# Moving one bf16 permutation from VectorE to GpSimd, behind a gate, and two matmuls ahead of a stage

## The chip, the cores and the metric

One core of a Trainium2 chip. The metric is device time of one execution in microseconds (us). Engines: PE is TensorE (PEld its weight loads), DVE is VectorE, ACT is ScalarE, POOL is GpSimd, SP is SyncE, whose queue issues transposing DMAs and output stores.

## The reference

Two attention steps for 8 batches of 8 heads (sequence 576, head size 64, 32 packed queries), then a two-layer block with h*cos(h):

```python
p_packed = sm_attn(p, k, v)              # 32 packed queries per head
out = sm_attn(q, p_packed, p_packed)     # 576 queries per head
x = out.transpose(0, 2, 1, 3).reshape(B * S, H * D)
h = x @ w_in                             # 512 -> 2048
g = h * np.cos(h)
return g @ w_out                         # 2048 -> 512
```

## The kernel before

The kernel runs as a pipeline over batches. Batch s has a *stage* of 16 chunks: for each chunk, four hidden matmuls, a cosine on ScalarE and a product on VectorE. Output matmuls of batch s-1 are spread between the chunks as filler. Also in the stage, v of batch s+1 is permuted (`permute_v`) and multiplied with its attention weights (`pp`); `ppw` and `pw2` multiply that product with w_in. PSUM is the memory that matmuls write; a *bank* or *buffer* of it is free again when its content has been read. Ahead of each stage, ScalarE and VectorE normalise the probabilities (`a2n`) that the hidden matmuls read.

```python
A = ctx.enter_context(tc.tile_pool(name="psA", bufs=3, space=PSUM))   # ring of 3: chunks, pp, ppw
O = ctx.enter_context(tc.tile_pool(name="psO", bufs=2, space=PSUM))   # output banks
...
def permute_v(b, eng=G):
    vp[b] = vp_pool.tile([TP, C, H * D], BF16, name="vp", tag="vp")
    copy(eng, vp[b]..., bf["v", b]...)                # 96 x 3072, bf16
...
def normalise(b):
    ...                                                # ScalarE: exp(-ln(sum)) for y = 0, 1
    for y in range(2):
        V.scalar_tensor_tensor(out=a2n[b][:, y], in0=a2u[b][:, y], scalar=r1[b][:, y:y + 1],
                               in1=lns[b][:, y], op0=ALU.mult, op1=ALU.mult)
...
def h_mm(b, fc):                                       # one chunk
    ps = psa()
    for y in range(2):
        for e in range(2):
            nc.tensor.matmul(ps[:, e, 0:HS], PPW[b]..., a2n[b][:, y, ...], ...)
    ACT.activation(out=csv, in_=ps[:, :, 0:HS], func=AF.Sin, bias=PI_HALF)
    def rest():
        V.tensor_tensor(out=gT[b][:, fc, :]..., in0=ps[:, :, 0:HS], in1=csv, op=ALU.mult)
        ...
...
def slot(s, hooks, keep=0, heavy={}):                  # the stage
    left = filler[1] - keep
    out_eng[:] = (ACT,) if s > 1 else (V, ACT)
    for fc in range(NFC):
        h_mm(s, fc)()
        quota = ...                                    # share of `left` due after this chunk
        ...                                            # hooks of chunk fc run here, then fill(...)
...
ppw(2, 3, V)
normalise(2)
ACT.preload_act_table_set(SIN_SET)
fill(8)                                                # output matmuls
G.tensor_copy(out=gate, in_=xT["k", 4][0:1, 0, 0:1])   # holds the loads until k4 is transposed
for n, b in (("v", 4), ("q", 4), ("k", 5)):
    load(n, b)
fill(5)
slot(2, [(4, lambda: permute_v(3, V)), (7, lambda: pp(3, engs=(ACT, ACT))), (11, lambda: pw2(3))], 5, {11: 3})
```

The softmax here doesn't subtract the row's maximum and nothing guards it: scores larger than these inputs give would overflow.

## Time and profile before

250.03 us median of 6 runs (249.93 to 250.45). The first part of the profile's page gives busy time per engine and the share of the span:

```profile
PE 234.5 (94%) x2003; PEld 131.6 (53%) x2037; DVE 168.0 (68%) x254; ACT 166.9 (67%) x278; POOL 54.8 (22%) x68
```

PE bounds the kernel, so only time in which PE waits can be saved.

The timeline of batch 2's stage, before (columns: start in us, duration in us, engine, line, operation, output<-input and shapes, count; in brackets the engine's idle time and what ended it):

```profile
75.00 2.49 PEld L309 LDWEIGHTS <-gT 128*128 128x128 bf16 x13 [0.42 <-issue]
75.23 2.75 PE L309 MATMUL ot<-w_out_bf,gT 128*128 128x512 bf16 x12 [0.16 <-issue]
76.02 1.28 ACT L495 ACT_TABLE_LOAD   x1
77.20 1.54 DVE L243 SCALAR_TENSOR_TENSOR a2n<-a2u,r,lns 128x576 bf16<-128x576 bf16 x2
78.07 0.41 PE L256 MATMUL psA<-a2n,PPW 128*128 128x288 bf16 x2
78.80 0.41 PE L256 MATMUL psA<-a2n,PPW 128*128 128x288 bf16 x2 [0.32 <-DVE a2n L243]
...
83.92 0.95 DVE L77 COPY vp<-vbf 96x3072 bf16<-96x3072 bf16 x1
84.35 0.65 PE L256 MATMUL psA<-a2n,PPW 128*128 128x288 bf16 x4
84.78 2.08 DVE L263 TENSOR_TENSOR gT<-psA,cosT 128x576 bf16<-128x576 f32 x3
85.58 0.86 PE L183 MATMUL psA<-a1T,vp 96*128 96x64 bf16 x24 [0.58 <-DVE gT L263]
...
95.65 1.28 ACT L505 ACT_TABLE_LOAD   x1
```

At the head, the hidden matmuls need the two normalise instructions (L243, ending at 78.01 and 78.74): the first pair runs at 78.07, the second at 78.80. At `pp` (L183), the matmuls need a free buffer of the three-buffer PSUM ring. The one due is that of chunk 5, whose product was the first of the three at 84.78, ended at 85.53, and had the permutation in front of it in VectorE's queue.

To size a wait I take the distance between two matmul starts in the trace and subtract what the first costs when nothing waits (0.12 us for 288 columns, 0.213 for 512; uninterrupted neighbours in this trace start 0.122 and 0.216 us apart). That gives 0.73 us at the head (0.24 ahead of the first pair, 0.49 ahead of the second) and 0.74 us at pp. The two ScalarE table loads (76.02 and 95.65) bracket the stage: 19.63 us. I call this the *stage time*.

### The profile page before, as it was taken

What the parts mean: (1) busy time and instruction counts of PE and PEld (TensorE: products, weight loads), DVE (VectorE), ACT (ScalarE), POOL (GpSimd) and SP (SyncE); (2) the same over time, 40 slices, a digit from 0 to 9 for tenths busy, and PEclk for the clock granted to TensorE, in tenths of its full rate; (3) what the DMA queues carried; (4) which work ended last, traced back from release to release, by engine and by line L of the source; (5) the groups of instructions that cost most, each with busy time, mean ns of one, the idle gap of its engine ahead of it and who ended that gap; (6) DMA issues with size and microseconds to landing.
All of it is one profiled execution on the core that took longest, in us unless ns stands there. A gap on an engine that the chain in (4) does not pass through costs nothing.

```text
span 248.2 us, 5035 instructions
## 1 busy us (share of the span) xinstructions
PE 234.5 (94%) x2003; PEld 131.6 (53%) x2037; DVE 168.0 (68%) x254; ACT 166.9 (67%) x278; POOL 54.8 (22%) x68
## 2 busy tenths in 40 slices
PE   8878799999999899999999999999999999999993
PEld 3454374566544654475546554565456554665452
DVE  2549987789568967678857766678766774876110
ACT  2368799746566787888877777888787684873000
POOL 8333533240400044022313105030500000000000
PEclk9999999999999999999999999999999999999999
DMA  6999999999899999999989995989491113201133
GB/s 91 203 203 206 205 206 229 200 241 153 162 206 219 167 158 220 206 193 173 190 162 192 174 194 68 177 164 209 103 156 33 45 42 82 47 26 58 46 83 85
DMA packets 63175, 37.09 MB, mean 149 GB/s; under 512 B 35792, under 2 KB 58576, under 8 KB 63152
## 3 DMA queue, kind: packets, MB, share of 16 engines
q0 software_dynamic: 23152, 18.75, 49.5%
q1 hardware_dynamic: 39568, 17.83, 34.3%
q8 instruction: 16, 0.26, 0.4%
q10 hardware_dynamic: 432, 0.20, 0.4%
q14 instruction: 7, 0.06, 0.1%
HBM read 37.22 MB, written 9.44 MB: 188 GB/s over the span
## 4 chain that ended last, share of the span: by engine, by line
PE 75%; DMA 9%; DVE 7%; ACT 5%; issue 2%; SPq 0%; DVEq 0%; ACTq 0%
PE ot L309 42%; PE psA L256 19%; DMA qbf<-in_q_dram 7%; DVE gT L263 4%; PE psA L207 3%; PE ot L347 3%; PE psA L183 2%; ACT cosT L260 2%; DMA out_dram<-osb 2%; PE psA L129 2%; PE ot L295 1%; PE psA L233 1%; DVE PPW L77 1%; ACT ppT L75 1%; PE psA L104 1%
## 5 line engine op out<-in xcount | busy, mean ns | idle before, releaser
L309 PE MATMUL ot<-w_out_bf,gT 128*128 128x512 bf16 x482 | 127.4, 379 | 2.1 <-issue 1.3
L263 DVE TENSOR_TENSOR gT<-psA,cosT 128x576 bf16<-128x576 f32 x128 | 93.6, 755 | 26.5 <-ACT cosT L260 25.9
L260 ACT ACTIVATE cosT<-psA 128x576 bf16<-128x576 f32 x128 | 82.5, 652 | 28.0 <-PE psA L256 23.2
L256 PE MATMUL psA<-a2n,PPW 128*128 128x288 bf16 x512 | 83.8, 286 | 1.9 <-DVE PPW L77 0.4
L309 PEld LDWEIGHTS <-gT 128*128 128x128 bf16 x512 | 47.7, 98 | 43.2 <-issue 6.7
L256 PEld LDWEIGHTS <-PPW 128*128 128x128 bf16 x512 | 49.3, 98 | 35.2 <-issue 4.4
L77 DVE CAST PPW<-psA 128x1024 bf16<-128x1024 f32 (+1 forms) x23 | 26.9, 1176 | 11.6 <-PE psA L207 11.5
L267 POOL COPY joint<-gT 128x512 bf16<-128x512 bf16 x16 | 9.8, 614 | 88.5 <-DVE gT L263 88.5
L77 DVE COPY osb<-ot 128x512 f32<-128x512 f32 (+1 forms) x24 | 16.3, 679 | 17.5 <-PE ot L309 7.6
L75 ACT COPY osb<-ot 128x512 f32<-128x512 f32 (+1 forms) x13 | 7.3, 565 | 15.3 <-PE ot L309 10.6
L77 POOL COPY vp<-vbf 96x3072 bf16<-96x3072 bf16 x6 | 16.5, 2751 | 3.8 <-DMA vbf<-in_v_dram 3.8
L243 DVE SCALAR_TENSOR_TENSOR a2n<-a2u,r,lns 128x576 bf16<-128x576 bf16 x16 | 12.3, 814 | 7.3 <-ACT lns L241 7.3
L140 ACT ACTIVATE a<-psA 128x576 bf16<-128x576 f32 x16 | 10.3, 647 | 7.1 <-PE psA L129 7.1
L235 ACT ACTIVATE lns<-psA 128x576 f32<-128x576 f32 x16 | 10.2, 650 | 7.1 <-PE psA L233 6.5
L309 PE MATMUL ot<-w_out_bf,joint 128*128 128x512 bf16 x46 | 12.4, 379 | 0.1
L225 ACT ACTIVATE a2u<-psA,rs 128x576 bf16<-128x576 f32 x16 | 11.0, 737 | 1.4 <-PE psA L129 1.3
L75 ACT CAST ppT<-psA 64x128 bf16<-64x128 f32 x24 | 6.2, 260 | 7.2 <-DVE ppT L77 5.9
L207 PE MATMUL psA<-w_in_bf,ppT 64*32 64x512 bf16 x224 | 10.2, 381 | 0.0
L347 PE MATMUL ot<-wz 128*128 128x512 bf16 x23 | 8.7, 524 | 1.4 <-DVE wz L358 1.2
L241 ACT ACTIVATE lns<-lns 128x576 f32<-128x576 f32 x16 | 10.0, 676 | 0.0
L183 PEld LDWEIGHTS <-vp 96*128 96x128 bf16 x192 | 6.6, 98 | 2.2 <-issue 1.1
L77 DVE COPY kT<-psA 128x768 bf16<-128x768 bf16 x8 | 4.2, 552 | 5.2 <-PE psA L104 5.1
(72 smaller groups left out, 150.8 us busy)
## 6 DMA issues: line engine op xcount, KB each, us to landing
kbf<-in_k_dram POOLq DMA_DIRECT2D x8, 576.0 KB, 12.0
vbf<-in_v_dram POOLq DMA_DIRECT2D x8, 576.0 KB, 7.3
qbf<-in_q_dram POOLq DMA_DIRECT2D x8, 576.0 KB, 9.6
out_dram<-osb SPq DMA_DIRECT2D x24, 192.0 KB, 2.6
out_dram<-osb SPq DMA_DIRECT2D x22, 128.0 KB, 2.4
w_in_bf<-in_moe_w_in_dram POOLq DMA_DIRECT2D x4, 512.0 KB, 17.5
w_out_bf<-in_moe_w_out_dram POOLq DMA_DIRECT2D x4, 512.0 KB, 20.4
out_dram<-osb SPq DMA_DIRECT2D x26, 64.0 KB, 2.1
```

Source lines behind the costliest of these rows:

```text
L75: ACT.copy(out=out, in_=in_)
L77: eng.tensor_copy(out=out, in_=in_)
L140: ACT.activation(out=a1[b % 2][:, y, :, 0:TP].rearrange("p (e m) x -> p e m x", e=2), in_=ps[y][:, :, 0:HS].rearrange("p e (m x) -> p e m ...
L183: nc.tensor.matmul(ps[:, hp * 64:(hp + 1) * 64], vp[b][:, c, hp * 128:(hp + 1) * 128], a1T[b][0:TP, :, j, 32 * hp:32 * hp + 32], start=(j ...
L207: nc.tensor.matmul(ps[y][32 * x:32 * x + 32, :], ppT[b % 2][r, 2 * x + y, :], w_in_bf[r, x, n * 512:(n + 1) * 512], start=True, stop=True)
L225: ACT.activation(out=a2u[b][:, y].rearrange("p (e x) -> p e x", e=2), in_=ps[y][:, :, 0:HS], func=AF.Exp, scale=rs1[b][:, y:y + 1])
L243: V.scalar_tensor_tensor(out=a2n[b][:, y], in0=a2u[b][:, y], scalar=r1[b][:, y:y + 1], in1=lns[b][:, y], op0=ALU.mult, op1=ALU.mult)
L256: nc.tensor.matmul(ps[:, e, 0:HS], PPW[b][:, y, fc * 128:(fc + 1) * 128], a2n[b][:, y, e * HS:(e + 1) * HS], start=(y == 0), stop=(y == 1))
L260: ACT.activation(out=csv, in_=ps[:, :, 0:HS], func=AF.Sin, bias=PI_HALF)
L263: V.tensor_tensor(out=gT[b][:, fc, :].rearrange("p (e x) -> p e x", e=2), in0=ps[:, :, 0:HS], in1=csv, op=ALU.mult)
L309: nc.tensor.matmul(pss[c], w, w_out_bf[:, fc, :], start=(fc == 0), stop=(fc == NFC - 1))
L347: nc.tensor.matmul(wps, wz[:, 0:128], wz, start=True, stop=True)
```

## The change

GpSimd is otherwise idle here, so the permutation goes there. A one-element copy that reads the second normalised half holds GpSimd back until the normalise is over. Two output matmuls are taken from the stage and put ahead of it, so that 15 instead of 13 stand behind the normalise.

```diff
@@ -494,11 +494,13 @@
     normalise(2)
     ACT.preload_act_table_set(SIN_SET)
     fill(8)
+    G.tensor_copy(out=gate, in_=a2n[2][0:1, 1, 0:1])
+    permute_v(3)
     G.tensor_copy(out=gate, in_=xT["k", 4][0:1, 0, 0:1])
     for n, b in (("v", 4), ("q", 4), ("k", 5)):
         load(n, b)
-    fill(5)
-    slot(2, [(4, lambda: permute_v(3, V)), (7, lambda: pp(3, engs=(ACT, ACT))), (11, lambda: pw2(3))], 5, {11: 3})
+    fill(7)
+    slot(2, [(7, lambda: pp(3, engs=(ACT, ACT))), (11, lambda: pw2(3))], 5, {11: 3})
```

## The prediction

> **What bounds the kernel.** TensorE. The page's first part has PE busy 94% of a 248.2 us span, VectorE and ScalarE 67 to 68%; the chain that ended last is 75% PE; the clock is 1.00. In the timeline, matmuls follow each other almost without gaps (0.216 us per 128x512 output matmul, 0.122 us per 128x288 hidden matmul), so only a PE gap can be saved. Batch 2's stage (78 to 97 us) has two:
>
> 1. Head. The 13 output matmuls behind the normalise end at 78.04. The first two hidden matmuls (y=0) run at 78.07; the y=1 pair waits until 78.80 for the second normalise on VectorE, which ended at 78.74. Stall 0.49 us.
> 2. The pp matmuls of batch 3 could start at 84.84 and start at 85.58: 0.74 us. They need the PSUM buffer of hidden chunk 5, whose VectorE product ran at 84.78 to 85.53, because the 0.95 us v permutation sat before it (83.92 to 84.87). The waits view names it: PE L183 waited 0.6 us for DVE gT. In batch 3's stage, where GpSimd permutes, pp waits 0.07 us.
>
> **What the change does.** No PE work is added or removed. Two output matmuls move ahead of the stage: 15 instead of 13 behind the normalise, 29 instead of 31 spread inside. The permutation goes from VectorE (0.95 us) to GpSimd (2.75 us each in this trace). Its gate waits for the second normalise (78.74), its input v3 landed at 79.4, so it should run at about 79.5 to 82.3; pp needs it at about 84.6. GpSimd was idle there for 18 us. The loads of v4, q4, k5 behind it still wait for the k4 transpose that landed at 86.5, so they should move less than 1 us.
>
> Contention: the Trainium skill, "SBUF — State Buffer", section "Who interferes with whom", says a VectorE instruction with two SBUF inputs conflicts with a GpSimd instruction that reads SBUF, and one with a single SBUF input outside the 2-port modes does not. The normalise has two, so the gate keeps the copy off it; the products have one PSUM and one SBUF input. The trace agrees for those: under the GpSimd permutations at 29.2 and 51.7 us they took 0.745 to 0.758 us, as elsewhere. No overlap with a normalise is shown.
>
> **Sum, all on the critical path.** Head: the y=1 pair stays pinned at 78.80, but 0.43 us of matmuls fills the gap: -0.43. pp: chunk 5's product should end near 84.9, so pp starts 0.7 us earlier. Given back: fewer output matmuls per chunk tighten the three-buffer PSUM ring (ScalarE 0.65 plus VectorE 0.76 us per chunk, against about 0.82 of PE), and ScalarE's output copy comes one chunk earlier; I estimate 0.1 to 0.3 us of new stalls. Net about -0.9 us, kept to the end, since later stages are PE-bound and no matmul waits for a load there.
>
> **Predicted: 249.2 us, 8 in 10 between 248.6 and 249.9.** Chances: faster by over 2% 0.01, within 2% 0.98, slower by over 2% 0.01.
>
> **What would show it.** Right: v3's permutation on GpSimd at 79.5 to 82.3; products under it still 0.76 us; the y=1 stall at most 0.1 us; pp at about 84.9, stalled under 0.3 us; the stage's closing table load (95.65) about 0.9 us earlier and everything after shifted equally. Wrong: products lengthened under the copy; pp waiting for GpSimd; the v4, q4, k5 loads moved by over 1 us.
>
> **What would make it wrong.** The gap at pp is replaced by an equal wait on ScalarE's cosines, or the gain is absorbed later where a load or transpose sets the pace: then about 250 us.

## More of the kernel before

All executions quoted here are with a granted TensorE clock between 0.99 and 1.0.

Note the counts: 2037 weight loads but 2003 matmuls. Some 34 matmul records are missing from this trace, so a hole between two matmuls is a wait only if the weight loads show no matmul in it.

The experiments ran on three chips, each beside the kernel before, so the ratios compare better than the medians do.

## The result

249.25 us median of 6 runs (248.91 to 249.48), against 250.03 for the kernel before. The ratio is 0.9965, 95% interval 0.9952 to 0.9977. Ratios are the mean time of one kernel's fast runs over that of the other's in the same rounds, so not quite the ratio of the medians quoted. The interval ends below 1, so a small gain is shown.

The page of the changed kernel, busy time per engine:

```profile
PE 236.7 (96%) x2037; PEld 131.4 (53%) x2037; DVE 167.3 (68%) x253; ACT 166.8 (67%) x278; POOL 57.8 (23%) x70
```

PE's 94% has become 96%, but this is mostly not the change: all 2037 matmuls are recorded here, 34 more than before. DVE has lost one instruction and 0.7 us; POOL has gained two and 3.0 us. The timeline of the same stage, changed kernel, same columns:

```profile
75.50 2.92 PEld L309 LDWEIGHTS <-gT 128*128 128x128 bf16 x15 [0.42 <-issue]
75.51 3.41 PE L309 MATMUL ot<-w_out_bf,gT 128*128 128x512 bf16 x15
76.52 1.28 ACT L495 ACT_TABLE_LOAD   x1
77.70 1.54 DVE L243 SCALAR_TENSOR_TENSOR a2n<-a2u,r,lns 128x576 bf16<-128x576 bf16 x2
78.75 0.94 PE L256 MATMUL psA<-a2n,PPW 128*128 128x288 bf16 x4
79.30 0.10 PEld L256 LDWEIGHTS <-PPW 128*128 128x128 bf16 x1 [0.32 <-issue]
79.37 0.18 POOL L497 COPY gate<-a2n 1x1 bf16<-1x1 bf16 x1 [10.55 <-DVE a2n L243]
80.28 2.75 POOL L77 COPY vp<-vbf 96x3072 bf16<-96x3072 bf16 x1 [0.73 <-DMA vbf<-in_v_dram]
...
82.16 2.98 DVE L263 TENSOR_TENSOR gT<-psA,cosT 128x576 bf16<-128x576 f32 x4 [0.24 <-ACT cosT L260]
84.63 0.65 PE L256 MATMUL psA<-a2n,PPW 128*128 128x288 bf16 x4
85.19 0.86 PE L183 MATMUL psA<-a1T,vp 96*128 96x64 bf16 x24
85.30 1.47 DVE L263 TENSOR_TENSOR gT<-psA,cosT 128x576 bf16<-128x576 f32 x2 [0.16 <-ACT cosT L260]
...
95.04 1.28 ACT L507 ACT_TABLE_LOAD   x1
```

What to see. The stage time is 95.04 - 76.52 = 18.52 us, 1.11 less. The head wait is 0.30 us (the second pair again behind the second normalise, which ended at 79.24); the first pair no longer waits. The pp wait is 0.07 us: chunk 5's product, the last of the four from 82.16, ended at 85.14 with no permutation in front of it. So 0.73 + 0.74 has become 0.30 + 0.07, a saving of 1.10, which is the whole of the stage's 1.11. VectorE's products in the stage take 0.743 to 0.759 us in both kernels, also under the permutation. GpSimd began the permutation when v3 landed, 0.73 us after the gate had opened.

Why is the total only 0.78 us better by the medians? This profiled run opened its stage at 76.52, the one of before at 76.02, in code that the change does not touch. That offset of 0.50 us is complete at batch 1's first cosine (45.57 against 45.08), over 30 us before the first changed instruction. Behind the stage the two traces agree: 152.56 us from the closing table load to the end before, 152.61 after.

### The profile page after: what moved, and what is told of

The parts are those of the page before. It is cut to its first block, busy times and chain, and to the rows that moved or that the text cites. A ratio compares the mean times of both kernels' runs of the same rounds, so it can differ in the third digit from the quotient of the medians.

```text
span 247.7 us, 5071 instructions
## 1 busy us (share of the span) xinstructions
PE 236.7 (96%) x2037; PEld 131.4 (53%) x2037; DVE 167.3 (68%) x253; ACT 166.8 (67%) x278; POOL 57.8 (23%) x70
## 4 chain that ended last, share of the span: by engine, by line
PE 74%; DMA 15%; DVE 4%; ACT 2%; POOL 2%; issue 1%; DVEq 0%; POOLq 0%
PE ot L309 44%; PE psA L256 20%; DMA w_out_bf<-in_moe_w_out_dram 9%; DMA w_in_bf<-in_moe_w_in_dram 7%; PE psA L207 3%; DVE gT L263 2%; PE psA L129 2%; PE psA L183 2%; PE ot L295 1%; ACT cosT L260 1%; PE psA L233 1%; DVE PPW L77 1%; ACT ppT L75 1%; DVE a2n L243 1%; POOL kbf L84 1%
## 5 line engine op out<-in xcount | busy, mean ns | idle before, releaser
L309 PE MATMUL ot<-w_out_bf,gT 128*128 128x512 bf16 x512 | 133.3, 379 | 0.1
L77 POOL COPY vp<-vbf 96x3072 bf16<-96x3072 bf16 x7 | 19.3, 2751 | 5.1 <-DMA vbf<-in_v_dram 5.1
L309 PE MATMUL ot<-w_out_bf,joint 128*128 128x512 bf16 x48 | 13.0, 379 | 0.0
L84 POOL DMA_DIRECT2D vbf<-in_v_dram x8 | 6.2, 777 | 6.8 <-DVE vp L77 4.8
```

The source lines that it names most:

```text
L77: eng.tensor_copy(out=out, in_=in_)
L309: nc.tensor.matmul(pss[c], w, w_out_bf[:, fc, :], start=(fc == 0), stop=(fc == NFC - 1))
```

## The experiments

The theory: there are two PE waits, one at the head that two matmuls fill in part, and one at pp that comes from VectorE's queue; nothing else moves. Rivals: the gain is all relief of VectorE; the gain is all at the head; pp waited for the permuted v itself; the gate is what protects the normalise. All twelve experiments gave correct output. Waits are worked out from the traces as above; "behind" is the stretch from the closing table load to the end.

| run | time, us: median (range) | ratio | stage opens | head wait | pp wait | stage time | behind |
|---|---|---|---|---|---|---|---|
| before | 250.03 (249.93 to 250.45) | 1 | 76.02 | 0.73 | 0.74 | 19.63 | 152.56 |
| changed | 249.25 (248.91 to 249.48) | 0.9965 | 76.52 | 0.30 | 0.07 | 18.52 | 152.61 |
| e1_fill_only | 249.78 (249.46 to 249.86) | 0.9991 | 76.13 | 0.30 | 0.89 | 19.35 | 152.54 |
| e2_perm_only | 249.32 (249.07 to 249.63) | 0.9976 | 76.12 | 0.73 | 0.07 | 18.96 | 152.62 |
| e3_no_gate | 248.81 (248.77 to 249.23) | 0.9959 | 76.37 | 0.30 | 0.07 | 18.53 | 152.55 |
| e4_fill9 | 249.26 (249.07 to 249.70) | 0.9975 | 75.85 | 0.22 | 0.29 | 18.82 | 152.62 |
| e5_dve_fc2 | 249.70 (249.63 to 249.84) | 0.9978 | 76.16 | 0.73 | 0.46 | 19.35 | 152.55 |
| e6_dve_dummy | 249.76 (249.58 to 249.92) | 0.9980 | 75.91 | 0.30 | 0.89 | 19.35 | 152.61 |
| e7_pool_over_norm | 250.75 (250.45 to 251.22) | 1.0025 | 75.98 | 1.89 | 0.07 | 20.12 | 152.63 |
| e8_fill9_heavy | 249.11 (248.77 to 250.38) | 0.9961 | 76.63 | 0.22 | 0 | 18.48 | 152.61 |
| e9_act_osb | 248.99 (248.81 to 249.34) | 0.9952 | 76.67 | 0 | 0 | 18.27 | 152.63 |
| e10_after_again | 248.87 (248.77 to 249.30) | 0.9950 | 75.85 | 0.30 | 0.07 | 18.52 | 152.62 |
| e11_act_osb_again | 249.00 (248.94 to 249.28) | 0.9965 | 76.32 | 0 | 0 | 18.27 | 152.64 |
| e12_after_third | 248.94 (248.90 to 249.80) | 0.9967 | 75.98 | 0.30 | 0.07 | 18.52 | 152.62 |

How to read it: the "behind" column is constant to 0.1 us and the "stage opens" column scatters over 0.8 us, so the stage time is the sharp measure and a single total is a blunt one. Each stage time is from one profiled execution, but it came out the same in repeated kernels (18.52 three times, 18.27 twice). By totals alone e1, e5, e6 and e7 can't be told from the kernel before: their 95% intervals contain 1 (e1: 0.9979 to 1.0004). What they show rests on the traces. (In e4 and e8 the head wait lies behind chunk 0 and has another cause, told there. In e5 the wait in the pp column lies one chunk before pp.)

### e1: only the two matmuls

```diff
-    fill(5)
+    fill(7)
     slot(2, [(4, lambda: permute_v(3, V)), ...
```

> Only the two output matmuls are moved; the permutation stays on VectorE at chunk 4. 'Stage' is the time between the table load that opens batch 2's cosine stage and the one that closes it: 19.63 us before, 18.52 after. Theory (two independent PE gaps, 0.49 at the head and 0.74 at pp): the head gap shrinks to 0.3 or less, the pp gap stays at 0.6 to 0.8; stage 19.1 to 19.3, total 0.4 us under before (about 249.6). Rival A (the whole gain is the relief of VectorE): stage 19.5 or more, no change. Rival B (the whole gain is the head): stage 18.6, total as after.

The stage shortened by only 0.28 us, less than expected (19.35 against 19.1 to 19.3). The head wait fell as in the changed kernel, 0.73 to 0.30, but the pp wait grew from 0.74 to 0.89. In e1's timeline:

```profile
83.96 0.95 DVE L77 COPY vp<-vbf 96x3072 bf16<-96x3072 bf16 x1
84.82 2.08 DVE L263 TENSOR_TENSOR gT<-psA,cosT 128x576 bf16<-128x576 f32 x3
85.62 0.86 PE L183 MATMUL psA<-a1T,vp 96*128 96x64 bf16 x24 [0.73 <-DVE gT L263]
```

pp starts 9.49 us after the stage opened, against 9.56 before: it hangs on chunk 5's product, and that hangs on VectorE. What PE gains ahead of such a point it gives back there in waiting. Both single-cause rivals fall in the traced stage: this part alone does something, but not everything. The total (249.78, about 249.6 expected) does not settle it.

### e2: only the permutation

```diff
-    fill(7)
+    fill(5)
     slot(2, [(7, lambda: pp(3, engs=(ACT, ACT))), ...
```

(as an edit of the changed kernel)

> Only the permutation moves to GpSimd (with its gate); 13 output matmuls stay behind the normalise. Theory: head gap stays 0.49, pp gap falls from 0.74 to 0.1; stage 18.9 to 19.1, total about 249.4. Rival A: stage 18.5. Rival B: stage 19.6. The two parts should add: e1's saving plus e2's saving equal to 1.11 us of stage within 0.15.

```profile
84.45 0.65 PE L256 MATMUL psA<-a2n,PPW 128*128 128x288 bf16 x4
85.00 0.86 PE L183 MATMUL psA<-a1T,vp 96*128 96x64 bf16 x24
```

The stage shortened by 0.67 us: the pp wait went from 0.74 to 0.07, as expected, and the head wait stayed as before (at 0.73; the 0.49 of the expectation is the same misreading as in the prediction, see below). The parts do not add as closely as I had written: 0.28 + 0.67 = 0.95 against 1.11 together, 0.16 short. The missing 0.16 is the 0.15 that e1 gives back at pp. The order matters: the matmul move only pays in full once pp no longer hangs on VectorE.

### e3: no gate

```diff
-    G.tensor_copy(out=gate, in_=a2n[2][0:1, 1, 0:1])
     permute_v(3)
```

> After, without the gate on the second normalise. Theory: v3 lands 0.6 to 1.0 us after the normalise ends, so the permutation's own wait for v3 is the later one and the gate holds nothing back: permutation starts when v3 lands, normalise instructions 0.81 us each, stage 18.4 to 18.6, total as after within 0.15. Rival (the gate protects the normalise): the permutation starts before 77, a normalise instruction takes 1.5 us or more, the stage starts later and the total is above after by 0.5 us or more.

In mechanism as the theory expected: stage 18.53, normalise instructions of 0.81 us each. Two of its numbers missed: v3 landed 2.5 us after the normalise, not 0.6 to 1.0, and the total lies 0.44 us below the first of the changed kernel (0.06 and 0.13 below the later two, e10 and e12). GpSimd's row shows what held the permutation back instead:

```profile
81.58 2.75 POOL L77 COPY vp<-vbf 96x3072 bf16<-96x3072 bf16 x1 [13.22 <-DMA vbf<-in_v_dram]
```

It waited for v3's load, which landed well after the normalise (77.56 to 79.10 in this run). In this kernel the gate therefore costs nothing and, in the runs seen, holds nothing back. In all three traces of the changed kernel v3's load was the later event too, by 0.7, 2.3 and 2.2 us.

### e5: the permutation on VectorE two chunks earlier

```diff
-    slot(2, [(4, lambda: permute_v(3, V)), (7, ...
+    slot(2, [(2, lambda: permute_v(3, V)), (7, ...
```

(as an edit of the kernel before)

> The kernel before with the VectorE permutation two chunks earlier (behind chunk 2 instead of chunk 4), 13 output matmuls as before. Question: did pp wait for the permuted v itself, or for the product of chunk 5 that the permutation had pushed back on VectorE? Theory (product): v is ready about 1.5 us earlier, but products 3 to 5 all shift by most of 0.95 us, the PSUM ring holds the hidden matmuls back, and gaps of 0.4 to 0.8 us remain in chunks 5 to 7 and at pp together; stage 19.3 to 19.6. Rival (v itself): pp gap below 0.15 and no other gap; stage 18.9 to 19.0, as e2.

VectorE and then PE in e5:

```profile
82.37 0.94 DVE L77 COPY vp<-vbf 96x3072 bf16<-96x3072 bf16 x1
83.23 2.93 DVE L263 TENSOR_TENSOR gT<-psA,cosT 128x576 bf16<-128x576 f32 x4
```

```profile
84.03 0.65 PE L256 MATMUL psA<-a2n,PPW 128*128 128x288 bf16 x4 [0.29 <-DVE gT L263]
84.73 0.38 PE L309 MATMUL ot<-w_out_bf,gT 128*128 128x512 bf16 x1
84.95 0.65 PE L256 MATMUL psA<-a2n,PPW 128*128 128x288 bf16 x4
85.44 0.75 PE L183 MATMUL psA<-a1T,vp 96*128 96x64 bf16 x20
```

v was ready at 83.31, two microseconds before pp ran, and pp itself no longer waited. But the wait had moved to chunk 6, which needs the ring buffer of chunk 3, whose product the permutation had now pushed back to 83.98: 0.46 us. The rival (pp waits for v) would have had no wait left. The stage, 19.35, is 0.28 better than before's; a wait of 0.46 in place of 0.74 accounts for it. That is 0.39 worse than e2's, where VectorE doesn't permute.

### e6: the same VectorE work, useless, in the changed kernel

```diff
-    slot(2, [(7, lambda: pp(3, engs=(ACT, ACT))), ...
+    slot(2, [(4, lambda: V.tensor_copy(out=scr_b..., in_=scr_a...)), (7, lambda: pp(3, engs=(ACT, ACT))), ...
```

(with two scratch tiles and a memset of one of them on GpSimd in the stage before)

> After (v3 by GpSimd, 15 output matmuls ahead), with a copy of the same shape between two scratch tiles put back on VectorE where the permutation had been (behind chunk 4); nobody reads its result, the output is unchanged. Theory (VectorE's queue is what mattered): the pp gap returns as in e1, 0.8 to 0.95 us; stage 19.2 to 19.4. Rival (only v's readiness mattered): stage 18.5 as in after.

```profile
83.74 0.95 DVE L506 COPY scr_b<-scr_a 96x3072 bf16<-96x3072 bf16 x1
84.60 2.08 DVE L265 TENSOR_TENSOR gT<-psA,cosT 128x576 bf16<-128x576 f32 x3
85.40 0.86 PE L185 MATMUL psA<-a1T,vp 96*128 96x64 bf16 x24 [0.72 <-DVE gT L265]
```

e6 reproduces e1 to 0.01 us, although v had been permuted by GpSimd and nobody reads the copy's result: pp wait 0.89, stage 19.35. With e5 this settles that the 0.95 us in VectorE's queue, not v, was the cause at pp.

### e7: a GpSimd copy over the normalise

```diff
+    G.tensor_copy(out=gate, in_=lns[2][0:1, 1, 0:1])     # released by ScalarE's last exponential
+    G.tensor_copy(out=scr_b..., in_=scr_a...)            # the permutation's shape; scratch tiles and memset as in e6
     G.tensor_copy(out=gate, in_=a2n[2][0:1, 1, 0:1])
     permute_v(3)
```

> After, with a GpSimd copy of the permutation's shape between scratch tiles, released when the last exponential of the logarithms is written, so that it runs over the normalise; v3's own permutation follows behind its gate. Theory (VectorE instructions with two SBUF inputs wait for a GpSimd instruction that reads SBUF): a normalise instruction is held until the scratch copy ends, 1 to 2 us more until the second one ends, the head gap grows to 1.2 to 2.3 us, stage 19.5 to 20.5. Rival (no such conflict): both normalise instructions 0.81 us, stage 18.5 to 18.7.

GpSimd, VectorE and PE in e7:

```profile
76.22 2.74 POOL L501 COPY scr_b<-scr_a 96x3072 bf16<-96x3072 bf16 x1
```

```profile
77.17 3.13 DVE L245 SCALAR_TENSOR_TENSOR a2n<-a2u,r,lns 128x576 bf16<-128x576 bf16 x2
80.23 0.68 DVE L79 COPY osb<-ot 128x512 f32<-128x512 f32 x1
```

```profile
79.63 0.41 PE L258 MATMUL psA<-a2n,PPW 128*128 128x288 bf16 x2 [1.24 <-DVE a2n L245]
80.36 0.41 PE L258 MATMUL psA<-a2n,PPW 128*128 128x288 bf16 x2 [0.32 <-DVE a2n L245]
```

The pair of normalise instructions took 3.13 us instead of 1.54: the first one 2.40, ending at 79.57, 0.61 us after the scratch copy ended at 78.96; the second 0.81 as always. The head wait grew to 1.89 us and the stage to 20.12, 1.60 more than the changed kernel. This is what the gate guards against: had v3 landed before the normalise, an ungated permutation could have done this. It agrees with the Trainium skill, "SBUF — State Buffer", section "Who interferes with whom": a VectorE instruction with two SBUF inputs conflicts with a GpSimd instruction that reads SBUF. The products, with one PSUM and one SBUF input, keep their 0.76 us under the same kind of copy in every run here.

### e4: two more matmuls ahead

```diff
-    fill(7)
+    fill(9)
     slot(2, [(7, ...
```

> After, with two more output matmuls ahead of the stage: 17 behind the normalise, 27 inside. Theory: the 0.30 us left at the head in after goes, nothing comes back: stage 18.2 to 18.3, total about 249.0. Rival (fewer output matmuls inside tighten the PSUM ring): new gaps of 0.3 us or more between hidden matmuls, stage 18.5 or more.

The rival was right: the stage took 18.82 us, 0.30 longer than with 15. The wait for the normalise is gone, but three others have come: 0.22 us behind chunk 0, 0.29 at pp, and 0.16 further on, where a chunk starts at 91.68, just after VectorE's copy of a `pw2` product ended at 91.64; 0.67 in sum against 0.37 in the changed kernel, which accounts for the 0.30. The first has this cause:

```profile
78.30 0.56 PEld L256 LDWEIGHTS <-PPW 128*128 128x128 bf16 x4
78.49 1.28 DVE L77 COPY osb<-ot 128x512 f32<-128x512 f32 x2
78.52 0.65 PE L256 MATMUL psA<-a2n,PPW 128*128 128x288 bf16 x4
78.89 0.10 PEld L309 LDWEIGHTS <-gT 128*128 128x128 bf16 x1
79.23 0.38 PE L309 MATMUL ot<-w_out_bf,gT 128*128 128x512 bf16 x1
```

The first and the 17th of these output matmuls each complete an output bank. Both banks are then full, and their copies to SBUF stand behind the normalise in VectorE's queue. The next output matmul runs at 79.23, just after the first copy ended. The wait at pp comes from the ring. Chunk 5's product ends 2.13 us after the chunk's first matmul in both kernels, but PE is ready for pp after 1.90 us instead of 2.11, because one output matmul fewer stands between them.

### e8: a filler matmul ahead of pp

```diff
-    ..., (11, lambda: pw2(3))], 5, {11: 3})
+    ..., (11, lambda: pw2(3))], 5, {7: 1, 11: 3})        # and fill(9), as in e4
```

> An attempt to beat after: 17 output matmuls ahead of the stage as in e4, and one output matmul set ahead of pp at chunk 7 (extra weight there). Theory (e4's pp gap of 0.29 is a wait for chunk 5's product that other PE work can fill): pp gap below 0.1, head gap none, stage 18.4 to 18.6, that is 0.2 to 0.4 below e4 and about equal to after or 0.1 below. Rival (the ring sets the pace of the chunks themselves): new gaps between chunks, stage 18.8 as e4.

The pp wait is gone, stage 18.48. The wait for an output bank (0.22) stayed, and I had expected no head gap. About equal to the changed kernel, as expected. The listed waits are 0.15 fewer than the changed kernel's, the stage only 0.04 shorter: the trace has a new wait of 0.10 us between the two halves of the `pw2` matmuls.

### e9 and e11: the two output copies on ScalarE

```diff
     ACT.preload_act_table_set(SIN_SET)
+    out_eng[:] = ACT,
     fill(8)                                               # the rest as in e8
```

> e8 with the two output copies that follow the normalise on VectorE given to ScalarE, which sits idle there for about 2 us. Theory (in e4 and e8 the gain at the head was lost again because the first output matmul inside the stage waited 0.22 us for a PSUM bank whose copy stood behind the normalise on VectorE): that wait goes, no head gap is left, stage 18.1 to 18.35, total 0.2 us or so below after on the same chip. Rival (the stage is at its PE floor already): stage 18.45 or more.

ScalarE in e9; it sits idle between its table load and the first cosine, and takes the copies there:

```profile
76.67 1.28 ACT L495 ACT_TABLE_LOAD   x1
77.97 0.59 ACT L75 COPY osb<-ot 128x512 f32<-128x512 f32 x1
79.54 0.59 ACT L75 COPY osb<-ot 128x512 f32<-128x512 f32 x1 [0.99 <-PE ot L309]
```

The stage took 18.27 us with none of the earlier waits left, 0.25 less than the changed kernel, as expected. (0.37 of waits went, and the 0.10 at `pw2` that e8 shows came.) The total did not follow: 248.99 against 248.87 for the changed kernel on the same chip (e10).

> e9 once more, unaltered, because its stage was 0.25 us shorter in the profile while its total was not below after's. Theory (start-up differences hide it): stage 18.27 within 0.05 again, and over two submissions the mean total lies 0.1 to 0.3 us under after's. Rival (something ahead of the stage or behind it pays it back): the stretch behind the stage is longer than 152.65, or the total is again not below after's.

The stage was 18.27 again and the stretch behind it 152.64, but the total was again not below the changed kernel's (249.00 against 248.94), which I had named as the rival's sign. The traces put the difference ahead of the stage: it opened at 76.67 and 76.32 in e9 and e11, at 75.85 and 75.98 in the changed kernel beside them. That stretch has the same instructions in all of them, and the changed kernel itself opened at 76.52 once. Two things narrow it down. The late openings are complete early: batch 1's first cosine starts at 45.73 and 45.38 in e9 and e11, at 44.92 and 45.04 in e10 and e12, over 30 us before the first edited instruction. And they are hardly the luck of the two profiled executions. Nine of the eleven executions of e10 and e12 took 248.77 to 248.97; a stage 0.25 shorter would put as many of e9 and e11 under 248.75, and not one of their eleven was under 248.81. If the stage is as short in all of them, which only the profiled ones show, the rest is about 0.3 us longer in most. How the edit could do that, or whether something else differs, stays open, and I don't call e9 a faster kernel.

### e10 and e12: the changed kernel again

> The changed kernel, unaltered, for comparison on the same chip as e9, and to see how much the stretch ahead of the stage differs from run to run. Theory (the runs differ at the start, in code that the change does not touch): stage 18.5 within 0.05, the stretch behind it 152.6 within 0.1, whatever the total. Rival (the change made the start slower): the stage opens at 76.5 or later again, against 75.85 to 76.4 in most other runs.

> The changed kernel again, on the same chip as e11. Theory: stage 18.52, total 248.8 to 249.3, and the opening of the stage anywhere between 75.8 and 76.7.

Stage 18.52 in all three traces; totals 248.87 and 248.94, ratios 0.9950 and 0.9967, with the stage opening at 75.85 and 75.98. So the change did not make the start slower; its first profiled run had a late one. In the five traces with the latest openings (changed, e3, e8, e9, e11: 76.32 to 76.67) the chain of work up to 46 us runs through the load of w_out; in the other nine (75.85 to 76.16) it does not. So the scatter belongs to the stretch in which the first loads land; what makes them land late is not shown. The ratio is 0.995 to 0.997, in keeping with 1.11 us of 250 (0.44%). One thing to watch: in e10 and e12 v3 landed late, so the permutation ran at 81.15 and 81.24 and ended only about 0.6 us before pp started at 84.53 and 84.65.

## Why the prediction was right

The total (249.2 predicted; 249.25, 248.87 and 248.94 measured) and the range held, and so did the mechanism. That the first median agrees to 0.05 us is luck: its profiled run opened late, and the later two medians are 0.3 lower, in part because less was given back than I had allowed for. Point by point:

- **Bound and place: right.** All of the saving is in PE's waits of batch 2's stage; the stretch behind is unchanged within 0.1 us.
- **Head, "-0.43": right in size, wrong in its reading.** I had read that the 13 output matmuls end at 78.04 and put the wait at 0.49. One matmul record was missing, and I took the hole to be at the end of the group. The weight loads (13 from 75.00) against the matmuls (12 from 75.23) show it at the front. The matmuls ended 0.21 earlier, PE also waited ahead of the first pair, and the wait was 0.73. Two matmuls took 0.43 off that, as they would have off any wait that long, so "the y=1 stall at most 0.1 us" was wrong: 0.30 stayed.
- **pp, "0.7 us": right.** 0.74 became 0.07 (e2: 0.67 alone), and e5 and e6 show the mechanism: the product queue on VectorE, not v.
- **Given back, "0.1 to 0.3 us": wrong.** Nothing measurable came back at 15 matmuls: 0.73 + 0.74 - 0.30 - 0.07 = 1.10 of a stage saving of 1.11. The worry was real, but one step further on: at 17 (e4) the ring and the output banks gave back more than the head gained. So the stage gained 1.11 rather than 0.9.
- **Net, "-0.9 us": right within the scatter.** By medians the gain was 0.78, 1.13 and 0.98 us; by the traces the stage gained 1.11 each time.
- **Timing of the parts.** The permutation took 2.75 us on GpSimd, the products kept 0.76 us. On VectorE it takes 0.94 to 0.96 us in these traces. That agrees with the Trainium skill, "VectorE: DVE Perf Modes", section "Side-by-side: where the cycles go for N=2048 bf16": its 4x column, (3072/4 + 8 + 150 cycles)/0.96 GHz, gives an estimate of 0.96 us. The stage's close moved 0.61 us in the first profile and not "about 0.9", because it opened 0.50 later. The v4, q4 and k5 loads were issued 1.03 us later (88.64 for v4 against 87.61, 0.50 of it from the later opening), just over the "1 us" that I had named as a sign of error; nothing downstream waited for them, as the unchanged stretch behind shows.
- **Contention: right, and then shown by e7** for the case that the trace before could not show. In the changed kernel itself it never came up: v3 landed after the normalise in every trace.

## What to carry to other kernels

On a kernel bound by PE, price a helper instruction by the wait that it puts into the queue ahead of a buffer release, not by its length: here 0.95 us on VectorE cost PE 0.67 (e2) or 0.83 us (e6), 0.39 when queued two chunks earlier (e5), and 2.75 us on GpSimd cost none that the stage time shows. A move of filler work pays only up to the next point that hangs on another engine (e1), and too much of it makes new waits (e4). Compare a stretch bounded by two marks inside one trace when the effect is under half a per cent; the first 45 us of this kernel alone scatter by 0.8 us.

## What the Trainium skill lacked or had wrong

- "SBUF — State Buffer", section "Summary: rules for kernel authors": the conflict itself is as described (e7). The page says that the second one to issue fully blocks until the first finishes. The blocked normalise ended 0.61 us after the recorded end of the GpSimd copy, although it takes 0.81 us when run freely, so about 0.2 us of it appears to overlap with the blocked time. That page says nothing of it, and no run here shows which part overlaps; the profile gives spans on GpSimd only roughly, so the difference may be one of the record.
- "GPSIMD Engine Reference": no page gives the time of a bf16 copy on GpSimd; here 96x3072 took 2.75 us. The page's section "3.1 Elementwise — side-by-side cycle accounting" has 1.03 cycles per element for bodies with k ≤ 2 without saying what k counts. If a copy is one of them, 3072 elements at the 1.2 GHz of the page's table are an estimate of 2.64 us, 4% under the measured time.
- No page speaks of the run-to-run scatter with which a kernel's first loads land. Here the openings of this stage, all set by 45 us, lie between 75.85 and 76.67 us in 14 traces.
